# Loading q in two DMAs by heads, and spreading four k placements over eight steps

## Chip, cores and metric

The kernel runs on one core of one Trainium2 chip. The metric is the device time of one execution in microseconds (us). Three executions of the kernel before gave a median of 257.22 us, from 256.88 to 257.70. Engines are called by the names that the profile uses: PE is TensorE (matmuls), PEld its weight loads, DVE VectorE, ACT ScalarE, POOL GpSimd, SP SyncE.

## The reference

Block-sparse attention of 4 batches, 8 heads, 768 positions and head width 64, and behind it a gated feed-forward layer over all 3072 tokens.

```python
k_sum = k.reshape(B, H, nb, 32, D).max(axis=3)          # one summary key for 32 keys
v_sum = v.reshape(B, H, nb, 32, D).mean(axis=3)
scores_l = scale * q @ k^T, kept where |i - j| < 16      # a band of neighbours
scores_s = scale * q @ k_sum^T + log(32)
a = softmax(concat([scores_l, scores_s]));  x = a @ concat([v, v_sum])
# x as 3072 x 512
g = x @ w_gate;  val = x @ w_val                         # 512 -> 1536
out = x + sigmoid(x @ w_res) * ((gelu(g) * val) @ w_out)
```

## The kernel before

The work is cut into eight units of 384 tokens, two for each batch. A unit takes 12 steps `fo`; in each of them PE makes a 128x384 tile of `g` and one of `vv`, ACT takes the gelu of `g`, DVE multiplies it with `vv` into `gvT`. Scores and attention of the next unit are woven into the output stage of this one. Four PSUM banks go round for `g`, `vv` and the output tiles: when DVE is late with `gvT`, PE has no bank for a later tile.

Names in the profile lines: `tp` is a tile of transposes, `mt` the turned `mneg`, `kW` the placed keys and `ks` their block maxima, `vext` the v tiles, `vs` sums of v, `s` scores, `ao` and `xn` the attention output before and after it is normalised, `xp` the transposes of `xn`.

The start, in program order. All loads that convert to bf16 are issued by POOL, which also makes the mask tile `mneg` with four selects (code cut, cuts are marked):

```python
        k_sb[0] = k_tile()
        load_k(0, k_sb[0], 0, 2)                 # k, heads 0 to 3
        nc.gpsimd.affine_select(out=ident[:], ...)
        load_k(0, k_sb[0], 1, 2)                 # k, heads 4 to 7
        q_sb[0] = load_q(0, QJ)                  # q of the first half, all heads
        # ... constants on ACT and DVE
        v_loads(0, 0, 6)                         # six v tiles, one DMA each
        for cols, sign, base in (...):           # four selects
            nc.gpsimd.affine_select(out=mneg[0:QT, cols], ...)
        v_loads(0, 6, 7)
        load_w(w_gate, wg_src, 0)
        v_loads(0, 7, NT)                        # five more v tiles
        # ... then all the weights, and q of the second half among them
```

PE meanwhile follows its own list, in this order. `keep_warm(n)` is n matmuls on zeros whose result nobody reads:

```python
        keep_warm(12)
        k_step(0, 0, ps_mm, "mm"); k_step(0, 1, ps_mm, "mm")   # transposes of k
        keep_warm(6)
        k_step(0, 2, ps_mm, "mm")
        nc.tensor.transpose(mt[:], mneg[:], ident[:])          # needs mneg
        k_step(0, 3, ps_mm, "mm")
        keep_warm(5)
        tq = [turn_pair(q_sb[0], hp, ...) for hp in range(NP)] # transposes of q
        # ... scores; sums of v over blocks: vsum_mm(0, vs, 3, 8) needs v tile 7
```

The second place is unit 1, where k of batch 1 is turned on PE and placed: one copy on ACT, a max over 32 keys and three copies on DVE, for each of four head pairs `hp`.

```python
        def k_place(b, hp, tp):
            nc.scalar.copy(kW[b % 2][:, :, hp, 0:QT]..., tp...)
            k_blocks(b, hp)                      # DVE: tensor_reduce max, tensor_copy (kW<-ks)
            k_rims(b, slice(hp, hp + 1), nc.vector)   # DVE: two tensor_copy (kW<-kW)
        # ... in the loop over fo, behind the g and vv matmuls and gvT of this fo
                    if nb == 1:
                        if fo == 0:
                            tk = turn_all(k_sb[nb])
                        if fo < NP:
                            k_place(nb, fo, tk[fo])
```

The softmax here doesn't subtract the row's maximum and nothing guards it: scores larger than these inputs give would overflow.

## Time and profile before

| | before |
|---|---|
| span of the profiled execution | 255.5 us, clock 1.00 |
| PE busy | 246.8 us, 97% |
| DVE, ACT, POOL busy | 157.9, 126.9, 110.5 us |

The head of the profile page, busy time, and from its fourth part the chain of work that ended last, by engine:

```profile
PE 246.8 (97%) x2277; PEld 138.2 (54%) x2300; DVE 157.9 (62%) x350; ACT 126.9 (50%) x212; POOL 110.5 (43%) x155
...
PE 80%; DMA 10%; DVE 4%; POOL 3%; issue 2%; POOLq 0%; DVEq 0%
```

PE is the bottleneck. What can be won or lost is in its gaps, and those are short. So we look at instructions in order of time. The columns are: start, time taken, engine, line, operation, result <- inputs, shapes, count, and in brackets how long the engine was idle and what ended it. First POOL of the kernel before, at the start:

```profile
2.50 0.71 POOL L88 DMA_DIRECT2D k_sb<-in_k_dram  x1
3.21 0.78 POOL L96 DMA_DIRECT2D q_sb<-in_q_dram  x1
3.98 4.10 POOL L103 DMA_DIRECT2D vext<-in_v_dram  x6
8.00 0.92 POOL L183 TENSOR_SCALAR_AFFINE_SELECT mneg<-mneg 64x64 bf16<-64x64 bf16 x4
9.03 0.68 POOL L103 DMA_DIRECT2D vext<-in_v_dram  x1
10.57 0.77 POOL L161 DMA_DIRECT2D w_gate<-in_moe_w_gate_dram  x1 [0.86 <-DMA q_sb<-in_q_dram]
```

Two readings. `mneg` is complete at 8.92. And the issue of w_gate, the eleventh DMA, waits for the landing of q, the third: an issue waits for the DMA eight issues earlier. The program uses eight completion semaphores in turn for these loads; in the packed trace their numbers, 99 to 106, come round after every eighth load.

PE of the kernel before, same stretch and up to the end of the attention of unit 0:

```profile
9.07 0.23 PE L463 MATMUL mt<-ident,mneg 128*128 128x128 bf16 x1
...
10.88 0.87 PE L211 MATMUL tp<-ident,q_sb 96*64 96x96 bf16 x32
...
14.32 1.04 PE L265 MATMUL vs<-vext,bmat 64*32 64x256 bf16 x8
15.78 0.38 PE L265 MATMUL vs<-vext,bmat 64*32 64x256 bf16 x2 [0.42 <-DMA vext<-in_v_dram]
...
19.96 0.34 PE L360 MATMUL xp<-ident,xn 128*128 128x128 bf16 x3
...
35.55 0.82 PE L375 MATMUL g<-xT,w_gate 128*128 128x384 bf16 x4
36.61 0.82 PE L375 MATMUL vv<-xT,w_val 128*128 128x384 bf16 x4 [0.23 <-DMA w_val<-in_moe_w_val_dram]
```

PE turns `mneg` as soon as it is there, and turns q without a wait. It waits twice for data: for v tile 7 at 15.78, and for the last block of w_val at 36.61.

DVE of the kernel before, in unit 1 (steps fo 0 and fo 1):

```profile
55.75 0.55 DVE L381 TENSOR_TENSOR gvT<-ge,vv 128x384 bf16<-128x384 f32 x1
56.21 0.95 DVE L228 TENSOR_REDUCE ks<-kW 128x24 bf16<-128x768 bf16 x1
57.19 0.24 DVE L232 COPY kW<-ks 128x288 bf16<-128x288 bf16 x1
57.34 0.71 DVE L236 COPY kW<-kW 128x176 bf16<-128x176 bf16 x1
57.46 0.63 DVE L237 COPY kW<-kW 128x176 bf16<-128x176 bf16 x1
58.02 0.53 DVE L381 TENSOR_TENSOR gvT<-ge,vv 128x384 bf16<-128x384 f32 x1
```

and PE beside it:

```profile
57.65 0.81 PE L375 MATMUL g<-xT,w_gate 128*128 128x384 bf16 x4
58.60 0.81 PE L375 MATMUL vv<-xT,w_val 128*128 128x384 bf16 x4
...
63.36 0.81 PE L375 MATMUL vv<-xT,w_val 128*128 128x384 bf16 x4
64.14 0.81 PE L375 MATMUL g<-xT,w_gate 128*128 128x384 bf16 x4
```

Back to back, such groups of four start 0.65 us apart. Here they are 0.95 apart: `vv` of fo 3 waits 0.3 us for the second `gvT` above to end. Before it stand a whole placement, and in it two copies of 0.71 and 0.63 us, where the same copies take 0.20 us in other places.

### The profile page before, as it was taken

What the parts mean: (1) busy time and instruction counts of PE and PEld (TensorE: products, weight loads), DVE (VectorE), ACT (ScalarE), POOL (GpSimd) and SP (SyncE); (2) the same over time, 40 slices, a digit from 0 to 9 for tenths busy, and PEclk for the clock granted to TensorE, in tenths of its full rate; (3) what the DMA queues carried; (4) which work ended last, traced back from release to release, by engine and by line L of the source; (5) the groups of instructions that cost most, each with busy time, mean ns of one, the idle gap of its engine ahead of it and who ended that gap; (6) DMA issues with size and microseconds to landing.
All of it is one profiled execution on the core that took longest, in us unless ns stands there. A gap on an engine that the chain in (4) does not pass through costs nothing.

```text
span 255.5 us, 5803 instructions
## 1 busy us (share of the span) xinstructions
PE 246.8 (97%) x2277; PEld 138.2 (54%) x2300; DVE 157.9 (62%) x350; ACT 126.9 (50%) x212; POOL 110.5 (43%) x155
## 2 busy tenths in 40 slices
PE   6999999999999999999999999999999999999994
PEld 2565654565554565545554655546554665456543
DVE  5965876399477544767567544857567544854424
ACT  6776359276482338344482338244482337253320
POOL 8897452193345987265405986265404000000000
PEclk9999999999999999999999999999999999999999
DMA  5999999999913999979703999979703500240003
GB/s 80 178 147 174 198 202 208 188 143 200 142 25 93 170 107 143 119 143 168 130 14 97 173 111 156 102 141 166 129 15 78 136 0 3 50 139 0 0 3 123
DMA packets 98475, 29.34 MB, mean 115 GB/s; under 512 B 83592, under 2 KB 95312, under 8 KB 98352
## 3 DMA queue, kind: packets, MB, share of 16 engines
q0 software_dynamic: 68720, 14.76, 67.9%
q1 hardware_dynamic: 29728, 14.21, 24.9%
q8 instruction: 18, 0.29, 0.5%
q14 instruction: 9, 0.07, 0.1%
HBM read 29.36 MB, written 6.29 MB: 140 GB/s over the span
## 4 chain that ended last, share of the span: by engine, by line
PE 80%; DMA 10%; DVE 4%; POOL 3%; issue 2%; POOLq 0%; DVEq 0%
PE f L423 23%; PE vv L375 21%; PE g L375 21%; PE r L413 8%; DMA w_val<-in_moe_w_val_dram 5%; DMA w_gate<-in_moe_w_gate_dram 3%; PE ao L335 3%; DMA q_sb<-in_q_dram 3%; PE s L299 3%; POOL vext L103 1%; DVE th L429 1%; DVE o L432 1%; PE vs L273 1%; POOL w_val L161 1%; POOL w_gate L161 1%
## 5 line engine op out<-in xcount | busy, mean ns | idle before, releaser
L381 DVE TENSOR_TENSOR gvT<-ge,vv 128x384 bf16<-128x384 f32 x96 | 52.5, 551 | 50.6 <-PE vv L375 46.3
L380 ACT ACTIVATE ge<-g 128x384 f32<-128x384 f32 x96 | 47.0, 490 | 69.4 <-DVE gvT L381 36.4
L375 PE MATMUL vv<-xT,w_val 128*128 128x384 bf16 x384 | 78.7, 326 | 0.4 <-DMA w_val<-in_moe_w_val_dram 0.2
L375 PE MATMUL g<-xT,w_gate 128*128 128x384 bf16 x384 | 78.8, 326 | 0.1
L423 PE MATMUL f<-w_out,gvT 128*128 128x512 bf16 x262 | 62.7, 379 | 1.5 <-issue 1.1
L375 PEld LDWEIGHTS <-w_gate 128*128 128x128 bf16 x384 | 37.1, 98 | 26.6 <-issue 1.8
L375 PEld LDWEIGHTS <-w_val 128*128 128x128 bf16 x384 | 37.4, 98 | 25.4 <-DMA w_val<-in_moe_w_val_dram 0.6
L423 PEld LDWEIGHTS <-gvT 128*128 128x128 bf16 x276 | 25.7, 98 | 29.5 <-DMA w_out<-in_moe_w_out_dram 0.3
L103 POOL DMA_DIRECT2D vext<-in_v_dram x48 | 33.3, 738 | 13.5 <-DMA w_out<-in_moe_w_out_dram 5.8
L416 ACT ACTIVATE th<-r 128x512 f32<-128x512 f32 x24 | 13.5, 605 | 27.5 <-PE r L413 27.5
L429 DVE SCALAR_TENSOR_TENSOR th<-th,f 128x512 f32<-128x512 f32 (+2 forms) x26 | 16.6, 640 | 14.3 <-PE f L423 14.3
L321 DVE TENSOR_TENSOR P<-P,maskt 128x768 bf16<-128x768 bf16 x30 | 17.1, 573 | 11.1 <-ACT P L317 6.1
L285 POOL COPY vext<-vsum 32x1536 bf16<-32x1536 bf16 x12 | 17.2, 1463 | 13.6 <-DMA vsum<-vpart 13.4
L413 PE MATMUL r<-w_res,xT 128*128 128x512 bf16 x88 | 22.7, 380 | 0.4
L432 DVE SCALAR_TENSOR_TENSOR o<-th,xn 128x512 f32<-128x512 f32 (+2 forms) x26 | 18.2, 701 | 0.9
L355 DVE TENSOR_TENSOR xn<-ao,rz 128x384 bf16<-128x384 f32 x32 | 17.8, 558 | 1.1
L317 ACT ACTIVATE P<-s,bias_t 128x768 bf16<-128x768 f32 x17 | 15.3, 902 | 4.3 <-PE s L299 4.1
L117 POOL DMA_DIRECT2D k_nat<-in_k_dram x24 | 16.4, 734 | 1.9 <-DMA k_nat<-in_k_dram 1.2
L123 POOL DMA_DIRECT2D q_nat<-in_q_dram x18 | 15.9, 921 | 0.7 <-issue 0.7
L314 ACT ACTIVATE P<-s,bias_t 128x384 bf16<-128x384 f32 x30 | 15.7, 580 | 0.0
L228 DVE TENSOR_REDUCE ks<-kW 128x24 bf16<-128x768 bf16 x16 | 15.1, 944 | 0.0
L413 PEld LDWEIGHTS <-xT 128*128 128x128 bf16 x96 | 8.8, 98 | 9.9
(83 smaller groups left out, 170.5 us busy)
## 6 DMA issues: line engine op xcount, KB each, us to landing
out_dram<-o SPq DMA_DIRECT2D x23, 256.0 KB, 2.3
vext<-in_v_dram POOLq DMA_DIRECT2D x48, 64.0 KB, 6.3
q_nat<-in_q_dram POOLq DMA_DIRECT2D x18, 128.0 KB, 7.3
w_gate<-in_moe_w_gate_dram POOLq DMA_DIRECT2D x6, 256.0 KB, 7.8
w_val<-in_moe_w_val_dram POOLq DMA_DIRECT2D x6, 256.0 KB, 8.8
w_out<-in_moe_w_out_dram POOLq DMA_DIRECT2D x3, 512.0 KB, 14.0
k_nat<-in_k_dram POOLq DMA_DIRECT2D x24, 64.0 KB, 4.8
vext<-vext SPq DMA_DIRECT2D x6, 144.0 KB, 5.8
```

Source lines behind the costliest of these rows:

```text
L103: nc.gpsimd.dma_start(out=vext[b % 2][0:QT, t, :, 0:D], in_=v[b, :, t * QT:(t + 1) * QT, :].rearrange("h p d -> p h d"))
L117: nc.gpsimd.dma_start(out=k_nat[:, t].rearrange("p (h d) -> p h d", d=D), in_=k[b, :, t * QT:(t + 1) * QT, :].rearrange("h p d -> p h d"))
L285: eng.tensor_copy(vext[b % 2][96:128, lo:hi, :, 0:D], src)
L321: nc.vector.tensor_mul(Pf, Pf, maskt.unsqueeze(1).to_broadcast([128, 2 * HT, QT]))
L355: nc.vector.tensor_mul(xn, ao[:, :, :, 0:D], rz.to_broadcast([128, NSUB, 2, D]))
L375: nc.tensor.matmul(ps[:, 0:TU], w[:, ko, fo * 128:(fo + 1) * 128], st["xT"][:, ko, :], start=(ko == 0), stop=(ko == KO - 1), skip_group_ch ...
L380: nc.scalar.activation(ge[:], g[:, 0:TU], AF.Gelu)
L381: nc.vector.tensor_mul(gvT[:, fo, :], ge[:], vv[:, 0:TU])
L413: nc.tensor.matmul(r[:], st["xT"][:, ko, ss], w_res[:, ko, :], start=(ko == 0), stop=(ko == KO - 1))
L423: nc.tensor.matmul(st["f", sub][:], gvT[:, fo, ss], w_out[:, fo, :], start=(fo == 0), stop=(fo == FO - 1), skip_group_check=True)
L429: nc.vector.scalar_tensor_tensor(th[:, cs], th[:, cs], 1.0, f[:, 0:n], ALU.add, ALU.mult)
L432: nc.vector.scalar_tensor_tensor(o.rearrange("p (k d) -> p k d", d=128), th[:, cs].rearrange("p (k d) -> p k d", d=128), 0.5, x, ALU.mult, ...
```

## The change

Its intent: the transposes of q could begin with the first four heads while the rest is still on its way; and DVE, which has about 1.4 us for a placement on top of 0.55 for `gvT` in steps in which PE takes 1.3 us, should get every second step free.

```diff
-    def load_q(half, j):
+    def load_q(half, j, n):
         t = qk.tile([TU // j, H, j, D], BF16, tag="q_sb", name="q_sb")
-        nc.gpsimd.dma_start(
-            out=t.rearrange("p h j d -> p h (j d)"),
-            in_=q[0, :, half * TU:(half + 1) * TU].rearrange("h (p j) d -> p h (j d)", j=j))
+        for i in range(n):
+            hs = slice(i * H // n, (i + 1) * H // n)
+            nc.gpsimd.dma_start(
+                out=t[:, hs].rearrange("p h j d -> p h (j d)"),
+                in_=q[0, hs, half * TU:(half + 1) * TU].rearrange("h (p j) d -> p h (j d)", j=j))
@@ at the start
-        q_sb[0] = load_q(0, QJ)
+        q_sb[0] = load_q(0, QJ, 2)
@@ among the weights
-                q_sb[1] = load_q(1, QJ)
+                q_sb[1] = load_q(1, QJ, 1)
@@ unit 1
-                        if fo < NP:
-                            k_place(nb, fo, tk[fo])
+                        if fo in (0, 2, 4, 6):
+                            hp = (2, 0, 1, 3)[fo // 2]
+                            k_place(nb, hp, tk[hp])
```

## The prediction

> What bounds the kernel. TensorE is busy 246.8 of 255.5 us (busy table) and holds 80% of the chain of waits that ended last, at full granted clock: only its gaps are for sale, about 9 us, a third of them before 21 us (17.96 busy of the first 20.9, by stages). In the stage of k_place (52.1 to 70.7) it is idle 0.14 us by the same view, although that stage lasts 18.6 us against 15.7 for the next one: the rest is the extra transposes (1.55) and the value sums (0.8). The change can win tenths there.
>
> Part 1, q in two DMAs. In the timeline TensorE starts the q transposes at 10.88, straight after five warm-up matmuls (9.70 to about 10.8); q lands at about 10.29 (chain of waits). TensorE does not wait for q, so half of it earlier wins nothing.
> The cost is on GpSimd, which issues these DMAs. The q issue is 0.78 us, two k issues 0.83 and 0.71; two half q issues should be about 1.4, so +0.65 us before six v issues (0.68 each) and the four selects that make mneg (8.00 to 8.92). And GpSimd waits before an issue for the DMA eight issues earlier (the w_gate issue at 10.57 waits for q, eight before it). With one more DMA the sixth v issue waits for the second half of k (issued 2.50, slowest landing 5.8, so 8.3) instead of the first. It goes out near 8.55, and mneg is ready near 10.1. The Trainium skill says the same ("DMA: Bandwidth & Descriptors", Anatomy of one DMA): DMA engines do not wait on semaphores, the issuing sequencer does.
> TensorE transposes mneg at 9.07, between the third and fourth k transposes: it should now stall 0.6 to 1.1 us there, and all behind it slides. VectorE is booked back to back from 5.24 to 16.3 and does not move. The 0.42 us wait at 15.78 for a v tile absorbs some; 0.5 to 0.7 are left at 21 us. The 0.23 us wait for the last w_val load (36.61) absorbs more, if the weights land when they do now: the DMA queue is backlogged by about 5 us (issue to landing 5.4), so a GpSimd delay of 0.3 us does not starve it. Net +0.4 us, estimated.
>
> Part 2, k_place on every second fo. One placement costs VectorE about 1.4 us (reduce 0.95, three copies), with gvT 0.55 it is 1.9 per fo against 1.30 for TensorE's matmuls: VectorE falls behind over four fo and has caught up at 65. But TensorE shows one stall from it: vv of fo 3 at 58.60, 0.3 us, released by the end of the gvT of fo 1 (58.55). Ahead of that gvT stand the out steps of the unit before, the gvT of fo 0 and the first placement, whose copies took 0.71 instead of 0.20 us while GpSimd was issuing. The change keeps a placement right there, so this stall may stay; later gvT come earlier, which nobody waits for now. 0 to -0.3, I take -0.1.
>
> Sum: 257.2 + 0.4 - 0.1 = 257.5 us, range 256.6 to 258.6; chances: faster by over 2% 0.01, within 2% 0.98, slower 0.01.
>
> What would show it. Right: mneg selects end at 9.6 to 10.2; TensorE stalls before the mneg transpose; no wait at 15.78; first w_gate issue still near 10.6; w_val landing near 36.6; stage of k_place 18.3 to 18.6 us. Wrong: mneg still by 9.1, or TensorE waiting for q in before after all (then part 1 wins up to 0.5 us); the weights landing later; or PSUM banks handed out otherwise after the reordering, with new stalls.

## The result, and the profile after

The kernel after took 257.49 us (median of six, 257.20 to 258.00) against 257.07 for the kernel before in six executions of the same sessions. The ratio is 1.0015, 95% interval 1.0001 to 1.0030: the same, within 2%. Ratios here are the mean time of one kernel's runs over that of the other's of the same rounds, so not quite the ratio of the medians quoted. Executions over 1.5% slower than the fastest of the same kernel are left out of the means. A second measurement, among the experiments, gave 1.0001 (0.9987 to 1.0015). By medians that is a loss of 0.4 us in the first measurement and 0.2 in the second, by means 0.4 and 0.04; the upper ends of the intervals are 0.8 and 0.4 us. In time the loss is hardly to be told from none. The traces, which resolve hundredths, show what happened.

| | before | after |
|---|---|---|
| span of the profiled execution | 255.5 | 255.7 |
| `mneg` complete | 8.92 | 10.21 |
| PE starts to turn `mneg` | 9.07 | 10.27 |
| first transposes of xn | 19.96 | 20.66 |
| `vv` of fo 10, the first that needs the last w_val | 36.61 | 36.91 |
| first `g` of unit 1 | 52.16 | 52.48 |
| first scores of unit 2 | 70.73 | 70.96 |

The head of the page of the kernel after, and its chain by engine. The DMA share is gone from the chain, PE has it:

```profile
PE 247.4 (97%) x2277; PEld 138.3 (54%) x2300; DVE 159.1 (62%) x350; ACT 127.2 (50%) x212; POOL 110.6 (43%) x156
...
PE 92%; POOL 3%; DVE 2%; issue 2%; ACT 0%; POOLq 0%; DVEq 0%
```

POOL of the kernel after, at the start:

```profile
3.21 1.33 POOL L98 DMA_DIRECT2D q_sb<-in_q_dram  x2
4.53 3.43 POOL L105 DMA_DIRECT2D vext<-in_v_dram  x5
8.65 0.68 POOL L105 DMA_DIRECT2D vext<-in_v_dram  x1 [0.69 <-DMA k_sb<-in_k_dram]
9.33 0.88 POOL L185 TENSOR_SCALAR_AFFINE_SELECT mneg<-mneg 64x64 bf16<-64x64 bf16 x4
10.31 0.68 POOL L105 DMA_DIRECT2D vext<-in_v_dram  x1
10.98 0.77 POOL L163 DMA_DIRECT2D w_gate<-in_moe_w_gate_dram  x1
```

Two half issues take 1.33 us instead of 0.78. The sixth v issue is now the tenth DMA, so it waits for the second, the other half of k, and POOL stands idle for 0.69 us. The selects come behind it. (The wait for q before w_gate has gone in return.) PE of the kernel after:

```profile
10.27 0.23 PE L465 MATMUL mt<-ident,mneg 128*128 128x128 bf16 x1 [1.04 <-POOL mneg L185]
...
12.07 0.87 PE L213 MATMUL tp<-ident,q_sb 96*64 96x96 bf16 x32
...
15.52 1.26 PE L267 MATMUL vs<-vext,bmat 64*32 64x256 bf16 x10
...
20.66 0.34 PE L362 MATMUL xp<-ident,xn 128*128 128x128 bf16 x3
...
36.25 0.82 PE L377 MATMUL g<-xT,w_gate 128*128 128x384 bf16 x4
36.91 0.82 PE L377 MATMUL vv<-xT,w_val 128*128 128x384 bf16 x4
```

PE stalls 1.04 us before `mneg` and is 1.20 us late from there on (10.27 against 9.07). It turns q 1.19 us later than before, although the first half of q landed at 9.37 by its completion semaphore and the whole at 10.37. At the sums of v the ten matmuls run through: the wait of 15.78 is gone, and 0.70 us of lateness is left at 20.66. Between `g` and `vv` of fo 10 lie 0.66 us (36.91 - 36.25) instead of 1.06 (36.61 - 35.55): the wait for w_val is gone too and takes 0.40. What stays is 0.30 us.

One profile on each side could differ by that much for other reasons, so here is that start of `vv` of fo 10 in all profiles whose first 10 us are like the one or the other. With `mneg` on time as in before: 36.61, 36.64 and 36.34 (before, place alone, placement on odd steps). With `mneg` late: 36.91, 36.73, 36.79 and 36.95 (after, after again, q in two alone, tiny DMA). The groups do not overlap, and their means are 0.3 us apart.

DVE of the kernel after in unit 1, the same steps:

```profile
56.05 0.55 DVE L383 TENSOR_TENSOR gvT<-ge,vv 128x384 bf16<-128x384 f32 x1
56.52 0.95 DVE L230 TENSOR_REDUCE ks<-kW 128x24 bf16<-128x768 bf16 x1
57.50 0.78 DVE L234 COPY kW<-ks 128x288 bf16<-128x288 bf16 x1
...
58.37 1.00 DVE L383 TENSOR_TENSOR gvT<-ge,vv 128x384 bf16<-128x384 f32 x2
```

and PE beside it:

```profile
57.96 0.81 PE L377 MATMUL g<-xT,w_gate 128*128 128x384 bf16 x4
58.95 0.81 PE L377 MATMUL vv<-xT,w_val 128*128 128x384 bf16 x4 [0.18 <-DVE gvT L383]
...
63.72 0.81 PE L377 MATMUL vv<-xT,w_val 128*128 128x384 bf16 x4
64.36 0.81 PE L377 MATMUL g<-xT,w_gate 128*128 128x384 bf16 x4
```

The first stall is where it was: 0.99 us from `g` to `vv`. The next `gvT` does come at once (two in a row from 58.37), and nobody was waiting for that one. The second stall is gone: from `vv` of fo 6 to `g` of fo 7 it is 0.64 us instead of 0.78.

### The profile page after: what moved, and what is told of

It is laid out like the page before. It is cut to its first block, busy times and chain, and to the rows that moved or that the text cites. A ratio compares the mean times of both kernels' runs of the same rounds, so it can differ in the third digit from the quotient of the medians.

```text
span 255.7 us, 5804 instructions
## 1 busy us (share of the span) xinstructions
PE 247.4 (97%) x2277; PEld 138.3 (54%) x2300; DVE 159.1 (62%) x350; ACT 127.2 (50%) x212; POOL 110.6 (43%) x156
## 4 chain that ended last, share of the span: by engine, by line
PE 92%; POOL 3%; DVE 2%; issue 2%; ACT 0%; POOLq 0%; DVEq 0%
PE g L377 24%; PE vv L377 24%; PE f L425 23%; PE r L415 8%; PE s L301 3%; PE ao L337 3%; PE tp L213 1%; POOL vext L105 1%; PE vs L267 1%; PE vs L275 1%; PE wp L457 1%; DVE o L434 1%; DVE th L431 1%; PE xp L362 1%; POOL k_sb L88 1%
## 5 line engine op out<-in xcount | busy, mean ns | idle before, releaser
L434 DVE SCALAR_TENSOR_TENSOR o<-th,xn 128x512 f32<-128x512 f32 (+2 forms) x26 | 18.8, 723 | 0.9
```

Source lines behind the costliest of these rows:

```text
L434: nc.vector.scalar_tensor_tensor(o.rearrange("p (k d) -> p k d", d=128), th[:, cs].rearrange("p (k d) -> p k d", d=128), 0.5, x, ALU.mult, ...
```

## The experiments

All were timed against the kernel before in five rounds, in three groups of four; each group ran on one chip and shares its runs of before. A group's median of before was 257.07, 257.28 and 257.44 us, so times are compared within a group only. All results were correct. "Edit" is against the kernel named.

### Each half alone

q in two DMAs, placement as before (edit on after):

```diff
-                        if fo in (0, 2, 4, 6):
-                            hp = (2, 0, 1, 3)[fo // 2]
-                            k_place(nb, hp, tk[hp])
+                        if fo < NP:
+                            k_place(nb, fo, tk[fo])
```

> The kernel before with q in two DMAs alone. My theory (one more GpSimd DMA makes the sixth v issue wait for the second half of k, mneg comes 1.2 us later, TensorE stalls before the mneg transpose): mneg selects end near 10.2, TensorE is 1.2 us behind before at the mneg transpose, 0.7 behind at 20 us, 0.3 to 0.5 behind at 40 us; ratio to before 1.001 to 1.002 (+0.3 to +0.5 us), the whole of the change's loss or a little more. Rival A (the placement causes the loss): ratio 1.000, with the late mneg hidden by the waits at 15.8 and 36.6. Rival B (the difference is noise): ratio 1.000 here and in the next run.

Measured: 257.31 us against 257.07, ratio 1.0008 (0.9995 to 1.0021). PE turns `mneg` at 10.18 behind a stall of 1.02 us, is at 20.54 with xn and at 36.79 with `vv` of fo 10: 0.58 and 0.18 behind before. The mechanism is as stated, the remainder at 40 us smaller than expected. The interval of the time holds both 1.000 and the expectation, so by the times alone rival B, noise, is not excluded.

Placement alone (edit on before):

```diff
-                        if fo < NP:
-                            k_place(nb, fo, tk[fo])
+                        if fo in (0, 2, 4, 6):
+                            hp = (2, 0, 1, 3)[fo // 2]
+                            k_place(nb, hp, tk[hp])
```

> The kernel before with k_place on fo 0, 2, 4, 6 in the order 2, 0, 1, 3 alone. My theory: TensorE is the same up to 52 us, the stall before vv of fo 3 stays at about 0.3 us (it waits for the gvT of fo 1, which still stands behind one placement), the gap of 0.12 us before g of fo 6 goes; so -0.1 us, ratio 0.9990 to 1.0003. Rival A (the placement causes the loss): ratio 1.001 to 1.002.

Measured: 257.19 us, ratio 1.0002 (0.9990 to 1.0014). The start is that of before (`mneg` at 9.18, xn at 20.02, `vv` of fo 10 at 36.64). The stall before `vv` of fo 3 was only 0.13 us (0.78 from `g` to `vv`); the longest copy of the first placement was 0.56 us here. So the expected 0.3 us did not come; the second stall, which the expectation places before fo 6, did go (`vv` at 63.22, `g` of fo 7 at 63.87, 0.65 apart). Nothing here speaks for rival A, that the placement is the loss. That the stall changed with the length of one copy gave the reading of part 2 below.

### One more DMA without the split

Edit on before:

```diff
+    extra = const.tile([1, D], BF16, name="extra")
@@ at the start
+        nc.gpsimd.dma_start(out=extra[:], in_=q[0, 0, 0:1, :])
         q_sb[0] = load_q(0, QJ)
```

> The kernel before, q in one DMA, with one tiny DMA (64 numbers into a tile that nobody reads) issued before q. It has the one more issue and the shifted wait for the eighth DMA before, without the split of q and almost without traffic. My theory: the sixth v issue waits for the second half of k, mneg selects end near 10.1, TensorE stalls 1.0 to 1.2 us before the mneg transpose, ratio 1.0005 to 1.002, as q alone. Rival C (the split itself costs, by more packets or a later landing of q): mneg on time near 9, no stall, ratio 1.000.

Measured: 257.47 us, ratio 1.0008 (0.9996 to 1.0020), no more than q in two. POOL of this run:

```profile
3.20 0.51 POOL L175 DMA_DIRECT2D extra<-in_q_dram  x1
...
8.60 0.68 POOL L104 DMA_DIRECT2D vext<-in_v_dram  x1 [0.68 <-DMA k_sb<-in_k_dram]
9.28 0.88 POOL L185 TENSOR_SCALAR_AFFINE_SELECT mneg<-mneg 64x64 bf16<-64x64 bf16 x4
```

A DMA of 64 numbers makes the same hole of 0.68 us in front of the sixth v issue and the same late `mneg` (PE turns it at 10.21). So it is the count of DMAs and the time of one issue that delay `mneg`, not the split of q and not its traffic. Rival C, for the stall, falls.

### Taking the selects out of the way

Two ways. First, the sixth v issue behind the selects (edit on after):

```diff
-        v_loads(0, 0, 6)
+        v_loads(0, 0, 5)
         # four selects
-        v_loads(0, 6, 7)
+        v_loads(0, 5, 7)
```

> The kernel after, with the sixth v load issued behind the four mneg selects instead of ahead of them, so the selects don't stand behind its wait. My theory: the selects end at 8.9, TensorE doesn't wait for mneg, its q transposes start at 10.9 as before, the waits for the v tile near 15.8 and for the last w_val near 36.6 are back; total as place alone: ratio to before 0.9990 to 1.0005, so 0.3 to 0.5 us faster than after. Rival C (split or landing of q costs): still 1.001 to 1.002.

Measured: 258.50 us, ratio 1.0036 (1.0003 to 1.0070). This expectation failed. `mneg` was on time (PE turns it at 9.13 without a stall, q at 10.94), as the theory has it, but v tile 7 landed at 16.42 instead of 15.74. PE:

```profile
16.46 0.38 PE L267 MATMUL vs<-vext,bmat 64*32 64x256 bf16 x2 [1.04 <-DMA vext<-in_v_dram]
```

And then something that I had not thought of. Busy time by stretches; the third number from the right is the granted PE clock:

```profile
15.00:18.00 3.00, 1.96 (x45) 1.25 (x44) 1.93 (x3) 1.52 (x3) 3.00 (x5) 1.00 1.62 124
18.00:24.80 6.80, 6.80 (x84) 4.48 (x82) 3.16 (x9) 3.05 (x6) 5.58 (x8) 0.50 1.34 171
```

From 18.0 to 24.8 us PE ran at half its clock. Three of the six executions show it (mean clock 0.980 to 0.985, 259.28 to 260.81 us; the slowest of them is not in the ratio); the three at full clock took 256.74, 257.06 and 257.71 us, as before. So the run says nothing against the theory of the late `mneg`, but its ratio can't be used for it.

Second, the selects ahead of all v loads (edit on after: the loop of four selects moved up to directly behind the two q issues).

> The kernel after with the four mneg selects ahead of the v loads (behind the two q issues), so neither the extra issue nor its wait for k stands before them. My theory: selects end near 5.6, TensorE has no wait for mneg and turns q at 10.9 as before. Issues of v0 to v4 go out 0.9 later than after, which the k and q data still in the queue until 10.3 should hide; the v tile that TensorE waits for at 15.7 lands no later than in before. The loss of q in two DMAs is gone: ratio to before 0.9985 to 1.0003 (-0.4 to +0.1). If the landing of that v tile is late as in the run with v5 behind the selects (16.4 instead of 15.7), TensorE waits for it and the clock may drop as there: over 1.003. Rival C (the split itself costs): 1.001.

Measured: 257.44 us, ratio 1.0015 (0.9988 to 1.0043). PE turns `mneg` at 9.08 and q at 10.89. It waits 0.86 us for v tile 7, which landed at 16.19, and two of six executions had the half clock (259.23 and 259.46 us). The other four took 257.07 to 257.47, median 257.39, against 257.28 for before. Removing the stall for `mneg` won nothing that the times show: what PE gains it spends waiting for the v tile, and sometimes it pays with the clock.

Is that wait what lowers the clock? The same with more matmuls on zeros put ahead of it:

```diff
-        vsum_mm(0, vs, 3, 8)
-        keep_warm(1)
+        vsum_mm(0, vs, 3, 7)
+        keep_warm(4)
+        vsum_mm(0, vs, 7, 8)
```

> The run with mneg first whose clock was halved from 18 to 25 us in two of six executions, with three more warm-up matmuls, and the one that came behind it, put ahead of the sums that wait for the v tile near 16.2. My theory (TensorE's idle time there, 0.9 us in a stretch of small matmuls, is what lets the clock drop): full clock in all executions, each 256.7 to 257.5. If some execution still falls to 0.985, the idle time before the v tile isn't the cause.

Measured: 257.13 us against 257.44, ratio 0.9990 (0.9975 to 1.0005), all six executions between 256.91 and 257.70 with a clock of 0.998 or more. As expected. With five drops in the twelve executions without the filler, none in six would come by chance about once in 25 times, (7/12)^6 = 0.04; measured against the selects-first run alone, with two in six, it is (4/6)^6 = 0.09. That is support, not proof.

The length of the gap cannot be the whole of it. The kernel after stands still for 1.04 us before `mneg` (0.75 in the repeat), q in two alone for 1.02, the tiny DMA for 0.95, and none of their 22 executions has a mean clock below 0.998. What differs there is the work around the gap, and where the gap falls in time. The filler changed two things at once, the idle time and the share of full-size matmuls beside the small ones; which of them counts was not separated.

### Using q at once

The run with the selects first, with the q transposes ahead of the five warm-up matmuls:

```diff
-        keep_warm(5)
         tq = [turn_pair(q_sb[0], hp, turn_tile(q_sb[0], ps_mm, "mm")) for hp in range(NP)]
+        keep_warm(5)
```

> The run with mneg first, with the five warm-up matmuls moved from ahead of the q transposes to behind them: what q in two DMAs was for. My theory: TensorE turns q about 0.6 to 1.0 us sooner (near 10.0 for the first heads, near 10.5 for the last), scores start no sooner than the five warm-up matmuls allow, and the wait for the v tile near 15.7 and for the last w_val near 36.6 take back whatever is won: same ratio as the run with mneg first, within 0.001. Rival E (early q pays once TensorE can use it): 0.5 us faster than that run, ratio below 0.998.

Measured: 257.13 us against 257.28, ratio 0.9991 (0.9978 to 1.0004), five executions within 0.21 us at full clock. PE turned q at 9.95 and was no earlier at xn for it (20.43; the selects-first run can't be compared there, its clock was low). The ratio is outside 0.001 of that run's 1.0015, because that had the low clock; against its four full-clock executions (mean 257.33) it is 0.2 us faster, less than rival E asks for. By this run alone the value of early q stays open.

### The placement on odd steps

Edit on before:

```diff
-                        if fo < NP:
-                            k_place(nb, fo, tk[fo])
+                        if fo in (1, 3, 5, 7):
+                            hp = (2, 0, 1, 3)[fo // 2]
+                            k_place(nb, hp, tk[hp])
```

> The kernel before with k_place on fo 1, 3, 5, 7 (order 2, 0, 1, 3), so that the gvT of fo 1 stands ahead of the first placement. My theory of part 2 (the one stall, 0.3 us before vv of fo 3, comes from the placement at fo 0 standing before the gvT of fo 1; even fo keep it): that stall goes, the stage from the k transposes to the first scores is 0.3 to 0.4 us shorter than before; ratio 0.998 to 1.000. Rival D (VectorE's total work in the stage is what counts, not its place): same stall as on even fo, ratio as in the run with placement alone, 1.000.

Measured: 257.19 us against 257.28, ratio 0.9993 (0.9977 to 1.0010); profiled span 254.8. DVE of this run:

```profile
55.47 0.55 DVE L381 TENSOR_TENSOR gvT<-ge,vv 128x384 bf16<-128x384 f32 x1
56.35 0.55 DVE L381 TENSOR_TENSOR gvT<-ge,vv 128x384 bf16<-128x384 f32 x1 [0.33 <-PE vv L375]
56.84 0.95 DVE L228 TENSOR_REDUCE ks<-kW 128x24 bf16<-128x768 bf16 x1
57.83 0.77 DVE L232 COPY kW<-ks 128x288 bf16<-128x288 bf16 x1
```

and PE beside it:

```profile
57.38 0.81 PE L375 MATMUL g<-xT,w_gate 128*128 128x384 bf16 x4
58.03 0.81 PE L375 MATMUL vv<-xT,w_val 128*128 128x384 bf16 x4
```

One copy is stretched to 0.77 us here too, but the second `gvT` is already done, and `vv` of fo 3 follows its `g` after 0.65 us. The stage from the first `g` to the first scores of the next unit is 18.15 us, against 18.57 before and 18.48 after. Rival D falls: the place decides. All runs together, from one profile each:

| placement | run | longest copy in the first placement, us | stage, us |
|---|---|---|---|
| fo 0 to 3 | before | 0.71 | 18.57 |
| | q in two alone | 0.42 | 18.16 |
| | tiny DMA | 0.41 | 18.15 |
| fo 0, 2, 4, 6 | after | 0.78 | 18.48 |
| | after again | 0.78 | 18.48 |
| | q sooner | 0.78 | 18.49 |
| | place alone | 0.56 | 18.27 |
| | filler | 0.54 | 18.24 |
| | v5 behind the selects | 0.43 | 18.15 |
| | mneg first | 0.23 | 18.15 |
| fo 1, 3, 5, 7 | four runs | 0.52 to 0.77 | 18.15, all four |

The first stall comes when a copy in the first placement is stretched beyond some 0.43 us, with the old spread as with the new one. POOL is issuing the six loads of q_nat then (54.46 to 59.77 in before), and the traces tell more than that. In all thirteen runs with a stretched copy, it ends 0.02 to 0.07 us after the end of one of these issues: in before the issue ends at 58.02 and the two copies at 58.05 and 58.09, in after 58.22 and 58.28, with odd steps 58.54 and 58.60. With the selects first the copy meets only the end of the last issue and takes 0.23 us, and no copy of these placements after the issues takes more than 0.24. So a stretched copy is held until an issue ends, and how long it takes depends on when in that issue it starts. The Trainium skill, "SBUF — State Buffer", section "SBUF: two separate sides", says that VectorE in some modes and GpSimd share a pair of ports as an exclusive lock, and that the loser is blocked. The 0.2 us copies that take 0.4 to 0.8 and end with an issue fit that, but not the whole of an issue holds a copy: in before one ran from 57.19 to 57.43 at its usual 0.24 us while an issue went from 57.07 to 58.02. The traces show no ports, and no run took the issues away, so the ports as the cause are argued and not shown; that the copies end with the issues, and that odd steps are indifferent to it, is shown.

The candidate with q in one DMA, selects first and odd steps:

> Candidate for a better kernel: q in one DMA, mneg selects ahead of the v loads, placement on odd fo. My theory: start as before or up to 0.4 us sooner at 20 us, given back at the wait for the last w_val near 36.6; stage of k_place 0.3 to 0.4 shorter; ratio 0.998 to 0.9995, that is 256.5 to 256.9 us.

Measured: 257.19 us, ratio 0.9992 (0.9976 to 1.0008), stage 18.15. The ratio is as expected, the median above the 256.5 to 256.9 us. As far as the noise lets one see, no better than odd steps alone; the selects' place is worth nothing with q in one DMA, where they were in time anyway.

### After again, and the best version

The kernel after, unedited:

> The kernel after itself, unedited, beside the next three on one chip. Ratio to before again about 1.0015; clock never below 0.997, because TensorE is late by the time it reaches the v tile and doesn't wait for it. If it is below 1.000 the difference was between chips or noise.

Measured: 257.65 us against 257.44, ratio 1.0001 (0.9987 to 1.0015), clock 0.998 or more. The stall before `mneg` is there again (PE turns it at 10.12 behind 0.75 us), and the stage is 18.48. This gives neither the 1.0015 nor less than 1.000. The two ratios together say: about 0.2 us slower, with nothing and 0.4 us both within reach.

q sooner, selects first, odd steps, q in two DMAs:

> The run with mneg first and the q transposes ahead of the warm-up matmuls, with the placement on odd fo. My theory: the start as in that run (0.9991 there), and the 0.2 to 0.3 us stall before vv of fo 3 goes: ratio 0.997 to 0.999, spread over five runs small, clock full.

Measured: 256.83 us, ratio 0.9978 (0.9960 to 0.9996), clock 0.997 or more, stage 18.15. It is the only version whose interval lies clear below 1, 0.6 us below before by medians (256.83 against 257.44) and 0.8 below after in the same group. Five of six executions lie within 0.24 us, one at 257.64. With a dozen intervals of 95% looked at, one that just clears 1 is no strong evidence by itself; the trace, in which the stall in unit 1 is gone, supports it.

The same with q in one DMA (the call `load_q(0, QJ, 1)`):

> The same with q in one DMA: whether two DMAs pay where TensorE can use the first half at once. q whole lands near 10.3, the first half would be there at 9.4, so the first transposes wait about 0.3 us more, but the wait behind them (v tile or warm-up matmuls) takes that back. My theory: ratio within 0.0007 of the run with two DMAs, or better by the one issue saved. Rival E (early q pays): slower by 0.3 us or more, 0.0012.

Measured: 257.03 us, ratio 0.9984 (0.9968 to 1.0000). PE waited 0.7 us for q in all, against 0.2 with q in two, and reached the sums of v tile 7 at 15.98 against 15.88: 0.1 us is left of the earlier q. The ratios differ by 0.0006, within the expected 0.0007. In the profiled execution the last w_val landed at 37.39 instead of 36.58 and cost PE another 0.5 us; why it came later there stays open. Whether two DMAs are worth up to 0.2 us in that order can't be told from these runs.

## Why the prediction was right, point by point

The time, 257.49 for 257.5, is closer than the noise deserves. What counts is the sum.

- **q was not what PE waited for.** Right: with its first half there at 9.37, PE turned q at 12.07, behind the program's order. Where q was used at once, 0.1 us of it reached the v sums.
- **One more DMA on POOL delays `mneg`.** Right in both terms: issues +0.55 (1.33 against 0.78; predicted 0.65), wait for the second half of k 0.69; `mneg` complete at 10.21 (predicted near 10.1), PE stall 1.04 (predicted 0.6 to 1.1). The tiny DMA reproduces it without the split. The Trainium skill, "DMA: Bandwidth & Descriptors", section "Anatomy of one DMA", puts such waits on the issuing sequencer, and this trace agrees: the v issue starts at 8.65 behind an idle 0.69 us.
- **Two later waits take most of it back.** Right: late by 1.20 at `mneg`, 0.70 at 20.66 (predicted 0.5 to 0.7), 0.30 at 36.91 (predicted 0.4). Between runs that last number varies: 0.34 with the tiny DMA, 0.18 with q alone, 0.12 in the run of after again.
- **The first w_gate issue would stay near 10.6.** Wrong, it was 10.98: I left out that another v issue of 0.68 us stands between the selects and w_gate. The last w_val landed at 36.87 instead of 36.56 in this run, and at 36.58 in the repeat, so that delay did not show reliably. The prediction had named later weights as a sign against it; in this run PE did not stand still for them (`vv` of fo 10 at 36.91).
- **The stall in unit 1 would stay.** Right: 0.30 before, 0.34 after. The -0.1 for this part was measured (18.57 to 18.48), but it came where the prediction saw nothing to win. It held that PE shows one stall from the placement and that nobody waits for the later `gvT`. There was the second stall, 0.13 us before `g` of fo 7, and the new spread removed it; 0.04 went back to the first. Nor is the gain the spread's alone: with a copy of 0.41 or 0.42 us two runs with the old placement have next to no stall (18.15 and 18.16). So the size was right by luck; what moves this stage most is how long one copy is held while POOL issues.

What I did not foresee: that taking the stall away, the obvious repair, would expose PE to a longer wait for v tile 7 and to a half clock. Why that tile lands 0.4 to 0.7 us later in those runs, while the DMA queue moves about 150 GB/s all the while, is not settled. With the same order of issues on POOL as selects first, it landed at 15.80 and 15.81 in the two runs with q sooner and q in two, so the order alone does not do it.

## What to carry to other kernels

Count DMAs, not only bytes: with a ring of eight semaphores one more issue shifts every later wait by one, and work of the same engine that stands behind such a wait is late with it. An earlier load only pays where the consumer's own instruction order asks for it early, and lateness ahead of a data wait is mostly forgiven there, as an early arrival is mostly wasted. To take side work off the critical path, ask which product the next stage waits for first and put the side work behind that one; here spreading it evenly without moving it from that place left the stall of 0.3 us where it was.

## What the Trainium skill lacked or had wrong

- "TensorE: Matmul & The Clock Gate", section "HAM oscillation", gives the rule that there be no PE idle gaps over about 3.4 us. Here a single gap of 1.04 us (0.86 in another run), in a stretch of small matmuls in which PE was busy 1.96 of 3.00 us, was followed by half the clock for 6.8 us. That is from the two profiled executions; by the clock, five of the twelve executions of these kernels had it, at a cost of about 2 us in four of them and 3.6 in the fifth. The length is two of the windows of 3.413 us of which the page's section "What's actually happening" tells. Another gap, of 1.04 us before `mneg` in the kernel after (0.75 in the repeat), had no such effect in twelve executions. The page's section "A second HAM failure mode: psum-queue depth-cycling" does say that short idle times between groups of matmuls can make the clock go back and forth, but gives no length for them.
- "SBUF — State Buffer", section "SBUF: two separate sides", has no size for short VectorE copies beside DMA issues from GpSimd. Here copies of 0.20 to 0.24 us took 0.4 to 0.8 us and ended 0.02 to 0.07 us after an issue. The section has the lock held for the whole instruction; here a copy that lay in the first 0.36 us of an issue of 0.95 us ran at its usual 0.24 us. That the shared ports are the cause was not tested.
- No page that I used says that a program which hands out a fixed set of completion semaphores in turn couples an issue to the DMA that many places earlier (eight here: 0.86 us idle before w_gate in the kernel before, 0.69 before a v load after).
